# One order of work for a recurrent attention block and its gated layer: block loads as k, w, then v and r; the diagonal's first products ahead of the last key products; the fifth unit's key copies later

## The chip, the cores and the metric

The kernel runs on one core of one Trainium2 chip. The metric is device time in microseconds (us), from the start to the end of one execution. Each core has five engines with instruction streams of their own: TensorE (PE, matrix products), VectorE (DVE), ScalarE (ACT), GpSimd (POOL) and SyncE (SP, which here only issues transfers). Sixteen DMA engines move data between the chip's main memory (HBM) and the on-chip memory (SBUF). TensorE writes its results to a separate memory of eight banks (PSUM).

## What is computed

```
B, H, S, D = 4, 8, 768, 48
state = 0                                   # (B, H, D, D)
for t in range(S):
    kt, vt, rt, wt = k[:,:,t], v[:,:,t], r[:,:,t], w[:,:,t]
    cur   = outer(u * kt, vt)
    y[t]  = rt @ (state + cur)
    state = wt[..., None] * state + outer(kt, vt)
x   = y as (B*S, H*D) = (3072, 384)
h   = x @ w_in                              # (384, 2048)
out = (h * sigmoid(h)) @ w_out              # (2048, 384)
```

All data are float32. The first block is a linear attention whose state decays with `w` at every step; the second is a feed-forward layer with the SiLU function.

## The kernel before, in words

**Units.** The sequence is cut into six pieces of 128 steps and the batch into two pairs, which gives twelve units (`units`, line 66), numbered 0 to 11. For one unit the recurrence is unrolled as a tree: `tw` holds products of `w` over 1, 2, 4, ... 64 steps (`product`, line 404), the keys `tk` and queries `tr` are multiplied by them level by level (`grow_own`, `grow_keys`, `grow_queries`, lines 606 to 649), and TensorE makes scores at each level (`score_products`, line 682). Two levels at a time go to TensorE as a `burst` (line 782). The scores of the blocks of eight steps on the diagonal are made apart, on POOL by products (`block_bonus`, steps 0 to 7, line 488, all recorded as L490) and on DVE by sums (`block_sum`, recorded as L527). These sums take a way over HBM into the right layout (`block_move`, line 545).

**What a loop turn holds.** From unit 3 on, the loop at line 1428 runs the attention of unit i together with the second matrix product of unit i - 2 (`downs`, seven products of 16 matmuls each, `quarter`, line 1296, recorded as L1321) and the first matrix product of unit i - 1 (`ups`, twenty products of 16 matmuls each, `first_part`, line 1187, recorded as L1178). Both products are of the Strassen kind, with fewer products and more sums. `mix(i)` (line 958) writes this order out by hand: a list of 21 groups, each with some steps of the attention and the number of products of the feed-forward layer that follow it. Each engine takes its instructions in exactly this order (`manual_schedule`, line 78). I call the seven products q0 to q6 and the time from the `y_state` of one unit (PE, L840) to the next a unit's turn; the turn with the attention of unit i begins with the `y_state` of unit i - 1.

q0 to q6 add into three PSUM places in the order x, z, x, y, x, y, x (line 1312). A product that comes back to a place must wait until ACT (L1326) or DVE (L1329) has taken the earlier result from it, so q4 waits for ACT's copy of q2, q5 for that of q3, and q6 for DVE's sum of q4.

**Transfers.** `raw` has one room each for `w`, `r` and `k` of a unit from unit 4 on (`slot`, line 99), so a load of one unit waits until the earlier one's data were turned (`turn`, line 347, recorded as L361 on DVE). `load_blocks` (line 118, L127) brings a quarter of one of them with four transfers of 16 or 32 KB on SP; `block_loads` (line 955) lists four quarters for each of the names it is given, so that a name costs 16 transfers. `load_values` (L140, L147) has five. `load_rk` (L158) brings a second layout of `r`, `k` (issued by ACT) and `w` (by SP) for the diagonal. The attention's result goes from ACT's copies (`yt`, L866) over HBM to the layer's input: `x_out` (line 935, two transfers, L939) and `x_in` (line 942, one, L945), both issued by ACT, so that ACT's later copies stand behind them.

All transfers of SP and ACT share eight completion semaphores, which the framework gives out in turn; the built program makes each transfer wait until the one that had its semaphore before has landed, that is the one eight places ahead in the framework's order, whichever queue it is on.

**Around the change.** The lines that the change touches are 998 (unit 4), 1018 to 1038 (the groups of units 5 to 11) and 1050 to 1057 (which loads go behind which group). Before it, in a turn of a unit from 6 on, the loads of the next unit's `k` and half of its `r` stand in groups 1 to 3, and the other half of `r` and the `w` of the unit after the next stand in groups 12 to 15; in the turn of unit 5 the loads of `w` and `k` of unit 6 stand in groups 1 to 3, and `r` of unit 6 and `w` of unit 7 in groups 12 to 15. The queue of POOL in the last groups is: last key products (`go_on(i, 6)`, L639), `products_of(i + 1, 4, 5, 6)` (L407), then steps 0 to 3 of the diagonal.

Of the kernel before, what the change touches and what calls it, by code (L numbers as in the profile page):

```python
# [38 lines left out]
def kernel(  # L39
# [26 lines left out]
    units = [(n, b0) for n in range(S // L) for b0 in range(0, B, NB)]  # L66
# [885 lines left out]
    def both(fn, i, *args):  # L952
        return [(fn, i, b, *args) for b in range(NB)]
# [4 lines left out]
    def mix(i):  # L958
# [3 lines left out]
        def at(now, *steps):  # L962
            return steps if now else ()
# [4 lines left out]
        def sum_steps(j, *steps):  # L968
            return [(block_sum, j, x) for x in steps]
# [13 lines left out]
        if i < NPAIR:  # L983
            groups = [[*both(turn, i, "w"), (product, i, 0)],
                      [*both(turn, i, "k"), (odd_ones, i)], [*both(turn, i, "r"), (start_levels, i), (prepare_keys, i, 1)],
                      [(prepare, i, 1), *[(product, i, l) for l in range(1, NL)]],
                      [(burst, i, 1), (keep_level, i, 1)],
                      [(keep_level, i, 2), (go_on, i, 2)],
                      [(prepare, i, 3), (reverse_v, i), (bonus, i, 0), (bonus_sum, i, 0)],
                      [(bonus, i, 1), (burst, i, 3), (keep_level, i, 3), (bonus, i, 2)],  # L990
                      [(keep_level, i, 4), (go_on, i, 4), (bonus_sum, i, 1), (load_rk, i + 1), (load_u,)],
                      [(prepare, i, 5), (make_block_mask,), (bonus_spread, i)],
                      [(burst, i, 5), (keep_level, i, 5, 0), (keep_level, i, 6, 0), (go_on, i, 6), (bonus_write, i, (0,)), (keep_level, i, 5, 1), (keep_level, i, 6, 1), (bonus_write, i, (1,))], *end]
            groups = list(zip(groups, (1, 1, 0, 2, 1, 1, 1, 1, 1, 2, 2, 1, 1)))
        else:
            j = i - 1
            if i <= NPAIR:
                groups = [([*both(turn, i, "r"), (grow_own, i, 0), (x_out, j), *at(j >= NPAIR, (add_update, j))], 2),
                          ([*start(i), *bonus_steps(i, 4), (x_in, j), (reverse_v, i)], 1),
                          ([(grow_queries, i, 2), (sums_of_x, j, 0)], 1),  # L1000
                          ([(odd_keys, i, 2), (grow_keys, i, 2, False), (sums_of_x, j, 1)], 1),
                          ([(sums_of_x, j, 2), *sum_steps(i, 2), (prepare, i, 3), *bonus_steps(i, 5, 6, 7), (sums_of_x, j, 3, 4, 5, 6)], 2),
                          ([(burst, i, 3), (keep_level, i, 3)], 2),
                          ([*sum_steps(i, 3)], 1),
                          ([], 1),
                          ([*sum_steps(i, 4), (keep_level, i, 4)], 2),
                          ([(go_on, i, 4)], 1),
                          ([], 1),
                          ([*at(ahead, (load_rk, i + 1, (0, 1), nc.scalar)), (block_move, i, False), (block_move, i, True), *at(ahead, (load_rk, i + 1, (2,)))], 1),
                          ([], 1),  # L1010
                          ([(sums_of_x, j, 7)], 1),
                          ([(prepare, i, 5)], 2),
                          ([], 1),
                          ([(burst, i, 5), (keep_level, i, 5, 0), (keep_level, i, 6, 0), (go_on, i, 6), (block_turn, i), (block_write, i, 1)], 2),
                          ([(keep_level, i, 5, 1), (keep_level, i, 6, 1)], 1),
                          ([(block_write, i, 0)], 1),
                          (end[0], 2), (end[1], 0)]
            else:
                groups = [([*both(turn, i, "r"), (grow_own, i, 0), (x_out, j)], 2),
                          ([*at(j >= NPAIR, (add_update, j)), *start(i), *bonus_steps(i, 4), (x_in, j), (reverse_v, i)], 1),  # L1020
                          ([(odd_keys, i, 2), (grow_keys, i, 2, False), (grow_queries, i, 2), *sum_steps(i, 2)], 1),
                          ([(prepare, i, 3), *bonus_steps(i, 5), (sums_of_x, j, 0, 1)], 1),
                          ([(sums_of_x, j, 2), *bonus_steps(i, 6, 7), (sums_of_x, j, 3, 4, 5, 6)], 2),
                          ([(burst, i, 3), *sum_steps(i, 3), (keep_level, i, 3), *sum_steps(i, 4)], 2),
                          ([*at(ahead, (load_rk, i + 1, (0, 1), nc.scalar)), (block_move, i, False), (block_move, i, True), *at(ahead, (load_rk, i + 1, (2,)))], 1),
                          ([*at(ahead, *both(turn, i + 1, "w"))], 1),
                          ([(keep_level, i, 4)], 2),
                          ([(go_on, i, 4), *at(ahead, *products_of(i + 1, 0, 1, 2, 3))], 1),
                          ([], 1),
                          ([], 1),  # L1030
                          ([], 1),
                          ([(sums_of_x, j, 7)], 1),
                          ([(prepare, i, 5)], 2),
                          ([], 1),
                          ([(burst, i, 5), (keep_level, i, 5, 0), (keep_level, i, 6, 0), (go_on, i, 6), *at(ahead, *products_of(i + 1, 4, 5, 6)), (block_turn, i), (block_write, i, 1)], 2),
                          ([(keep_level, i, 5, 1), (keep_level, i, 6, 1)], 1),
                          ([(block_write, i, 0)], 1),
                          (end[0], 2), (end[1], 0)]

        if i == NPAIR:  # L1040
            groups[0][0][:0] = sum_steps(i, 0, 1)
# [4 lines left out]
        if i < NPAIR:  # L1046
            behind = [group for group, _ in groups[8:]]
            for at, group in enumerate(behind):
                group += loads[at * len(loads) // len(behind):(at + 1) * len(loads) // len(behind)]
        elif ahead:  # L1050
            blocks = block_loads(i + 1, "wkr")
            head, tail = (blocks[0:8], blocks[8:]) if i == NPAIR + 1 else (blocks[4:10], blocks[10:])
            tail += block_loads(i + 2, "w") if i + 2 < len(units) else []
            for at, some in ((1, head[0:3]), (2, head[3:5]), (3, head[5:]), (12, [(load_values, i + 1), *tail[0:1]]),
                             (13, tail[1:3]), (14, tail[3:4]), (15, tail[4:])) if i > NPAIR else ((0, blocks[0:3]), (1, blocks[3:6]), (2, [*blocks[6:8]]), (3, [(load_values, i + 1)]),
                             (12, blocks[8:9]), (13, blocks[9:10]), (14, blocks[10:11]), (15, blocks[11:])):
                groups[at][0].extend(some)
        return groups
# [421 lines left out]
```

## Time and profile before

| what | us |
|---|---|
| median of 3 runs (lowest, highest) | 585.47 (584.42, 585.62) |
| the profiled execution: its own time | 585.87 |
| its span, first to last instruction | 584.0 |
| PE busy | 561.5 (96% of the span) |
| DVE busy | 482.8 (83%) |
| POOL busy | 384.4 (66%) |
| ACT busy | 270.2 (46%) |
| mean granted PE clock | 0.994 |

The turns of units 5 to 11 begin at 211.71, 260.90, 304.01, 347.99, 391.09, 437.72 and 480.36 us of the span, and the last `y_state` is at 522.95. A turn is thus 49.2, 43.1, 44.0, 43.1, 46.6, 42.6 and 42.6 us long.

In the lists by time, a row gives the start in us, the time from the start of the first to the end of the last of its instructions, the engine ("q" behind it: its instruction queue, which issues transfers), the line, what is written from what, and how many instructions are merged. In brackets stands the engine's idle time before the row and what ended it.

### The profile page before, as it was taken

How to read it: one execution, taken by the hardware profiler on the slowest of the kernel's cores; microseconds unless marked ns; L12 is line 12 of the kernel's file. 1: busy time of each engine (PE TensorE's matmuls, PEld its weight loads, DVE VectorE, ACT ScalarE, POOL GpSimd, SP SyncE). 2: the span in 40 equal slices, each digit the busy share in tenths (PEclk: the TensorE clock that was granted, in tenths of full speed). 3: DMA queues.
4: the chain of work that ended last, by engine and by line, in shares of the span. 5: the costliest groups of instructions: out<-in, count | busy, mean ns of one | idle time of the engine just before them, and what ended most of it. 6: DMA issues, size and time to landing. Idle time of an engine off the chain costs nothing.

```text
span 584.0 us, 18864 instructions
## 1 busy us (share of the span) xinstructions
PE 561.5 (96%) x7782; PEld 520.7 (89%) x7782; DVE 482.8 (83%) x748; ACT 270.2 (46%) x604; POOL 384.4 (66%) x447
## 2 busy tenths in 40 slices
PE   8989999999999898899999999998999999999997
PEld 8767776698899898899998999998999999899997
DVE  6979799998899998789989889889779989872350
ACT  5679694531531472274273274272274272271330
POOL 5998778447799997767867767865757857710000
PEclk9999999999999999899999999998999999999999
DMA  9957775344445443455555554455365452102000
GB/s 227 307 113 199 176 245 94 47 85 104 94 84 83 108 85 61 110 86 97 115 80 100 108 85 90 108 81 100 78 108 92 92 96 56 36 5 55 28 4 25
DMA packets 206485, 57.59 MB, mean 99 GB/s; under 512 B 186048, under 2 KB 198208, under 8 KB 206400
## 3 DMA queue, kind: packets, MB, share of 16 engines
q1 hardware_dynamic: 196272, 44.01, 38.6%
q10 hardware_dynamic: 10128, 12.39, 8.1%
q8 instruction: 61, 1.00, 0.8%
q14 instruction: 24, 0.20, 0.1%
HBM read 47.14 MB, written 9.18 MB: 96 GB/s over the span
## 4 chain that ended last, share of the span: by engine, by line
PE 59%; DVE 13%; SPq 9%; POOL 7%; DMA 5%; issue 4%; ACT 1%; ACTq 1%; DVEq 0%; POOLq 0%
PE p_o L1321 19%; PE p_o L1178 12%; PE p_h L1178 8%; SPq L127 8%; PE p_h L1071 5%; PE p_m L1260 4%; POOL tk L639 2%; PE p_sc L697 2%; PE p_h L1321 2%; DVE temps L1292 2%; DMA raw<-in_w_dram 2%; POOL w_in_sb L260 2%; DVE score L715 2%; DVE block_sums L527 1%; DVE tr L621 1%
## 5 line engine op out<-in xcount | busy, mean ns | idle before, releaser
L639 POOL TENSOR_TENSOR tk<-tk,tw 128x256 f32<-128x256 f32 x128 | 96.1, 771 | 39.3 <-ACT tk L609 27.9
L1321 PE MATMUL p_o<-own,temps 128*128 128x192 f32 x528 | 90.3, 331 | 3.6 <-ACT partial L1326 3.5
L1321 PEld LDWEIGHTS p_o<-own,temps 128*128 128x128 f32 x528 | 87.6, 193 | 4.9 <-ACT partial L1326 4.5
L1178 PE MATMUL p_o<-xt,w_in_sb 128*64 128x128 f32 x1152 | 72.1, 273 | 0.7 <-POOL w_in_sb L1117 0.7
L407 POOL TENSOR_TENSOR tw<-tw 128x256 f32<-128x256 f32 (+6 forms) x83 | 42.7, 515 | 38.7 <-DVE tw L361 18.6
L1071 PE MATMUL p_h<-xt,w_in_sb 128*128 128x256 f32 x288 | 66.1, 384 | 1.7 <-POOL w_in_sb L260 1.6
L1321 PE MATMUL p_o<-w_out_sb,gt 128*128 128x192 f32 x340 | 62.1, 337 | 5.8 <-DVE ob L1329 5.1
L1178 PEld LDWEIGHTS p_o<-xt,w_in_sb 128*64 128x64 f32 x1152 | 64.7, 137 | 0.9 <-POOL w_in_sb L1117 0.9
L1321 PEld LDWEIGHTS p_o<-w_out_sb,gt 128*128 128x128 f32 x340 | 56.6, 194 | 8.1 <-DVE ob L1329 6.5
L1071 PEld LDWEIGHTS p_h<-xt,w_in_sb 128*128 128x128 f32 x288 | 53.6, 190 | 10.0 <-POOL w_in_sb L260 2.4
L490 POOL TENSOR_TENSOR ruk<-tokens_rk 128x384 f32<-128x384 f32 x48 | 53.5, 1134 | 3.8 <-DMA tokens_rk<-in_k_dram 3.8
L621 DVE TENSOR_TENSOR tr<-tr,tw 128x512 f32<-128x512 f32 x61 | 52.6, 863 | 0.7
L1326 ACT COPY partial<-p_o 128x192 f32<-128x192 f32 x33 | 10.5, 318 | 84.2 <-PE p_o L1321 59.3
L1292 DVE TENSOR_TENSOR temps<-gt 128x512 f32<-128x512 f32 (+1 forms) x48 | 44.6, 966 | 0.0
L648 POOL TENSOR_TENSOR tk<-tk,tw 128x256 f32<-128x256 f32 x32 | 25.2, 817 | 22.8 <-DVE tk L361 22.8
L609 ACT COPY tk<-tk 128x256 f32<-128x256 f32 x52 | 20.9, 402 | 40.0 <-POOL tk L639 31.2
L1202 ACT ACTIVATE gt<-p_o 128x512 f32<-128x512 f32 x45 | 26.0, 601 | 20.1 <-PE p_o L1178 20.1
L715 DVE COPY_PREDICATED score<-mask,p_sc 128x512 f32<-128x512 int8 x42 | 31.3, 801 | 2.3 <-PE p_sc L697 1.9
L1326 ACT COPY ob<-p_o 128x192 f32<-128x192 f32 x11 | 3.5, 319 | 62.9 <-PE p_o L1321 51.3
L1321 PE MATMUL p_o<-w_out_sb,temps 128*128 128x192 f32 x176 | 30.5, 327 | 0.9 <-ACT partial L1326 0.9
L1321 PEld LDWEIGHTS p_o<-w_out_sb,temps 128*128 128x128 f32 x176 | 28.8, 190 | 1.2 <-ACT partial L1326 1.2
L1205 DVE TENSOR_TENSOR p_h<-p_h,gt 128x512 f32<-128x512 f32 x27 | 18.7, 694 | 12.6 <-ACT gt L1221 12.3
(240 smaller groups left out, 1307.5 us busy)
## 6 DMA issues: line engine op xcount, KB each, us to landing
w_out_sb<-in_moe_w_in_dram SPq DMA_DIRECT2D x6, 768.0 KB, 7.3
w_out_sb<-in_moe_w_out_dram SPq DMA_DIRECT2D x4, 768.0 KB, 7.5
own<-in_moe_w_out_dram SPq DMA_DIRECT2D x4, 768.0 KB, 6.4
tokens_w<-in_w_dram SPq DMA_DIRECT2D x8, 384.0 KB, 5.2
turned<-yt ACTq DMA_DIRECT2D x16, 192.0 KB, 2.6
xt<-turned ACTq DMA_DIRECT2D x8, 384.0 KB, 3.4
tokens_rk<-in_r_dram ACTq DMA_DIRECT2D x7, 384.0 KB, 4.2
tokens_rk<-in_k_dram ACTq DMA_DIRECT2D x7, 384.0 KB, 5.7
```

Source lines behind the costliest of these rows:

```text
L127: nc.sync.dma_start(out=room[(2 * e + a) * 32:(2 * e + a + 1) * 32, :, g, 0:d1 - d0], in_=src[b0:b0 + NB, e::2, t0:t0 + 32, d0:d1].rearran ...
L407: engine.tensor_tensor(out=up, in0=t[:, :, 0::2], in1=t[:, :, 1::2], op=ALU.mult)
L490: mul = lambda out, one, two: nc.gpsimd.tensor_tensor(out=out, in0=one, in1=two, op=ALU.mult)
L621: nc.vector.tensor_tensor(out=odd, in0=odd, in1=tw[i][l][:, :, 0::2][:, :, :, None].to_broadcast([128, Q, L >> (l + 1), c]), op=ALU.mult)
L639: nc.gpsimd.tensor_tensor(out=out, in0=have, in1=odd_products(i, l, b, *blocks), op=ALU.mult)
L648: nc.gpsimd.tensor_tensor(out=have, in0=have, in1=odd_products(i, l, b, [2, NP * ni]), op=ALU.mult)
L715: nc.vector.copy_predicated(out=dst, mask=masks[l][:, :, None].to_broadcast([128, NB, NP, ni, c]), data=sc[e].rearrange("p (b q) (i c) -> ...
L1071: nc.tensor.matmul(p_h[:, a, :], lhsT=w_in_sb[:, c, f * 128:(f + 1) * 128], rhs=xt[i][:, c, :], start=(a == 0 and c == 0), stop=(a == 1 an ...
L1178: nc.tensor.matmul(p[h:h + PD, q, :], lhsT=left[:, f:f + PD], rhs=right, start=first and q == 0, stop=q == 3, skip_group_check=True)
L1202: nc.scalar.activation(out=g(f, t), in_=have, func=AF.Silu)
L1292: nc.vector.tensor_tensor(out=out, in0=one, in1=two, op=op)
L1321: nc.tensor.matmul(p, lhsT=left(f), rhs=right[:, f, :], start=which in (0, 1, 3) and f == 0, stop=f == FH - 1, skip_group_check=True)
```

## The change

- For units 5 to 10 the loads of the next unit come in the order `k`, `w`, then values, then `r`. All of `k` and `w` (32 transfers) stand in groups 1 to 3, and the values and all of `r` (5 and 16) in groups 12 to 15. The `w` of the unit after the next is no longer loaded a turn ahead. The block loads of a turn are then 48 in each of the turns 5 to 10; before they were 64 in turn 5, 48 in the turns 6 to 9 and 32 in turn 10.
- The turning of the next unit's `w` on DVE moves from group 7 to group 9, behind `go_on(i, 4)` and just ahead of the products of `w` that read it.
- On POOL step 0 of the next unit's diagonal moves ahead of the last key products, `go_on(i, 6)`; the products of `w` of levels 4 to 6 move from behind these to the end, behind the diagonal's steps 1 to 3.
- For unit 5 alone, the copies of odd keys, the key products and the sums of level 2 move one group later (behind q3), and `prepare(i, 3)` goes from group 3 to group 4, behind the third of the sums of x; for units 6 to 11 these keep their order.
- For unit 4 a step that was empty there is taken out.

```diff
-                groups = [([*both(turn, i, "r"), (grow_own, i, 0), (x_out, j), *at(j >= NPAIR, (add_update, j))], 2),
+                groups = [([*both(turn, i, "r"), (grow_own, i, 0), (x_out, j)], 2),
...
+                soon = i > NPAIR + 1
+                keys_2 = [(odd_keys, i, 2), (grow_keys, i, 2, False), *at(soon, (grow_queries, i, 2)), *sum_steps(i, 2)]
+                keys_3 = [(prepare, i, 3), *bonus_steps(i, 5)]
...
-                          ([(odd_keys, i, 2), (grow_keys, i, 2, False), (grow_queries, i, 2), *sum_steps(i, 2)], 1),
-                          ([(prepare, i, 3), *bonus_steps(i, 5), (sums_of_x, j, 0, 1)], 1),
-                          ([(sums_of_x, j, 2), *bonus_steps(i, 6, 7), (sums_of_x, j, 3, 4, 5, 6)], 2),
+                          ([*at(not soon, (grow_queries, i, 2)), *at(soon, *keys_2)], 1),
+                          ([*at(soon, *keys_3), *at(not soon, *keys_2), (sums_of_x, j, 0, 1)], 1),
+                          ([(sums_of_x, j, 2), *at(not soon, *keys_3), *bonus_steps(i, 6, 7), (sums_of_x, j, 3, 4, 5, 6)], 2),
...
-                          ([*at(ahead, *both(turn, i + 1, "w"))], 1),
+                          ([], 1),
                           ([(keep_level, i, 4)], 2),
-                          ([(go_on, i, 4), *at(ahead, *products_of(i + 1, 0, 1, 2, 3))], 1),
+                          ([(go_on, i, 4), *at(ahead, *both(turn, i + 1, "w"), *products_of(i + 1, 0, 1, 2, 3))], 1),
...
-                          ([(burst, i, 5), (keep_level, i, 5, 0), (keep_level, i, 6, 0), (go_on, i, 6), *at(ahead, *products_of(i + 1, 4, 5, 6)), (block_turn, i), (block_write, i, 1)], 2),
+                          ([(burst, i, 5), (keep_level, i, 5, 0), (keep_level, i, 6, 0), *at(ahead, *bonus_steps(i + 1, 0)), (go_on, i, 6), (block_turn, i), (block_write, i, 1)], 2),
...
-                          (end[0], 2), (end[1], 0)]
+                          ([*at(ahead, *bonus_steps(i + 1, 1, 2, 3)), *at(ahead and i > NPAIR, *products_of(i + 1, 4, 5, 6))], 2),
+                          (end[1], 0)]
...
-            blocks = block_loads(i + 1, "wkr")
-            head, tail = (blocks[0:8], blocks[8:]) if i == NPAIR + 1 else (blocks[4:10], blocks[10:])
-            tail += block_loads(i + 2, "w") if i + 2 < len(units) else []
-            for at, some in ((1, head[0:3]), (2, head[3:5]), (3, head[5:]), (12, [(load_values, i + 1), *tail[0:1]]),
-                             (13, tail[1:3]), (14, tail[3:4]), (15, tail[4:])) if i > NPAIR else ((0, blocks[0:3]), (1, blocks[3:6]), (2, [*blocks[6:8]]), (3, [(load_values, i + 1)]),
+            blocks = block_loads(i + 1, "wkr" if i <= NPAIR else "kwr")
+            for at, some in ((1, blocks[0:3]), (2, blocks[3:6]), (3, blocks[6:8]), (12, [(load_values, i + 1), *blocks[8:9]]),
+                             (13, blocks[9:10]), (14, blocks[10:11]), (15, blocks[11:])) if i > NPAIR else ((0, blocks[0:3]), (1, blocks[3:6]), (2, [*blocks[6:8]]), (3, [(load_values, i + 1)]),
```

## The prediction

> **What bounds the kernel now.** I read the page's table of busy time first (PE at 96% of the span), then looked in the list of PE's work by time for idle stretches, then at whoever ended each.
>
> ```profile
> PE   561.5 (96%) x7782; PEld 520.7 (89%) x7782; DVE 482.8 (83%) x748; ACT 270.2 (46%) x604; POOL 384.4 (66%) x447
> ```
>
> PE's list, turns 5, 7, 9 and 10 in that order:
>
> ```profile
> 229.70 2.87 PE L1321 MATMUL p_o<-w_out_sb,temps 128*128 128x192 f32 x16 [0.95 <-ACT partial L1326]
> 235.17 4.55 PE L1321 MATMUL p_o<-w_out_sb,gt 128*128 128x192 f32 x16 [2.60 <-DVE ob L1329]
> ...
> 314.21 8.07 PE L1321 MATMUL p_o<-own,temps 128*128 128x192 f32 x48 [1.27 <-ACT partial L1326]
> ...
> 402.26 9.75 PE L1321 MATMUL p_o<-own,temps 128*128 128x192 f32 x48 [2.25 <-ACT partial L1326]
> ...
> 446.48 7.96 PE L1321 MATMUL p_o<-own,temps 128*128 128x192 f32 x48
> 457.45 2.87 PE L1321 MATMUL p_o<-w_out_sb,gt 128*128 128x192 f32 x16 [0.41 <-DVE ob L1329]
> ```
>
> PE waits only in the first half of a turn: in turns 7 and 9 before q2, for ACT's copy of q0; in turn 5 before q5 and q6; and before q6, for DVE, by 0.41, 0.40 and 0.41 us in turns 6, 8 and 10 and by 1.24 us in turn 11. The row at 402.26 also runs slow: 9.75 us where turn 10 takes 7.96. The windows' table tells why; its first number behind the length is PE's busy time, and PEclk stands behind POOL's:
>
> ```profile
> 399.97:403.39 3.42, 1.17 (x8) 1.13 (x8) 3.39 (x6) 1.50 (x7) 3.42 (x5) 1.00 0.69 121
> 403.39:406.80 3.41, 3.41 (x12) 3.41 (x11) 3.37 (x8) 0.69 (x4) 1.60 (x2) 0.50 0.61 142
> ```
>
> After a stretch in which PE was busy for 1.17 of 3.42 us, the clock was 0.50 in the next. The same happened in turn 5 (0.96 busy, then 0.50), not in turn 7 (2.14 busy, then 1.00).
>
> Why is ACT late in turn 9? ACT's list and SP's list:
>
> ```profile
> 393.28 2.36 ACT L866 COPY yt<-p_m 48x512 f32<-48x512 f32 x4 [0.98 <-PE p_m L861]
> 398.52 3.33 ACTq L939 DMA_DIRECT2D turned<-yt  x2
> 401.89 0.32 ACT L1326 COPY partial<-p_o 128x192 f32<-128x192 f32 x1 [6.25 <-DMA raw<-in_w_dram]
> ...
> 385.37 5.39 SPq L127 DMA_DIRECT2D raw<-in_r_dram  x8
> 390.86 9.92 SPq L127 DMA_DIRECT2D raw<-in_w_dram  x16
> 400.88 8.28 SPq L127 DMA_DIRECT2D raw<-in_k_dram  x16
> ```
>
> The copies of `yt` end at 395.64, but the two stores behind them (x_out) issue at 398.52 and 401.54: each shares a semaphore with a load of `w` that SP is still issuing. The built program names them, the 9th and the 13th of the 16 loads of `w`. ACT's copy of q0 stands behind, and PE behind that.
>
> **The change part by part.** The sum is made against the profiled execution, 585.87 us, which is 0.40 above the median.
>
> *Order of loads, turns 6 to 9 (start).* Behind the values SP now issues 16 loads of `r`; the 8 + 16 of `r` and `w` become 16. In the built program x_out waits for the 11th and the 14th of them. In turn 9 an `r` load took 5.39 / 8 = 0.67 us of issue; the 14th goes at 385.37 + 13 x 0.67 = 394.1 and lands some 2.1 us later (the median of the page's row for `r`), at 396.2. That is 0.6 us behind the copies of `yt` and before q0 ends (397.25), so ACT is ready. Turn 9 loses its 2.25 us wait and the slow clock, 9.75 - 7.96 = 1.79: 4.04 us. Turn 7 loses 1.27. In turns 6, 8 and 10 x_out is late too, but PE does not wait for it. Bounds: all of the 5.31, or only half of it if landings slip by 2 us; I take all, since the queue is 8 loads (5 us) shorter at this point.
>
> The Trainium skill (TensorE: Matmul & The Clock Gate, section Why this matters for your kernels) lets the clock fall only for idle gaps of over about 3 us; by it the 2.25 us of turn 9 would cost no clock and the sum would be 1.79 us smaller. The trace does not agree: 0.50 was granted after a gap of 2.25 us.
>
> *What takes its place.* `x_in` now waits for the 4th load of `k` in turns 6 to 10 (in turn 10 it waited for the 2nd, by the built program). In turn 10 the first went 9.04 us after the `y_state` (446.76 after 437.72), the 4th 1.35 later, plus 2.1 to land: 12.5. ACT's copy of q2 stands behind and must be done when q3 ends, 14.1 after the `y_state` (three products to 454.28 from 446.48, less one). Slack 1.2 us: cost 0, up to 1 us per turn if a landing takes 4 us, as `vq` does on the page.
>
> *The w loads between k and ACT's load_rk.* In turns 6 to 10 there are now 32 loads before it instead of 24, as turn 5 already had; load_rk of `k` waits for the 14th `w`, the 30th load. Turn 5 issued its 32 at 0.53 us (221.72 to 238.82), so the 30th goes 9.0 + 29 x 0.53 = 24.5 after the `y_state` and lands at 26.6; with 0.56 us of issue ACT goes on at 27.2. In turn 10 ACT's next copy began at 465.36, 27.6 after, and PE did not wait. Cost 0 by this, 0.45 by turn 5, whose long issue of 1.80 us left a PE wait of 0.45. Five turns, 0 to 2.25; I take 0.1 each, 0.5.
>
> *Turning w later.* 1.29 us on DVE move behind L621 (425 in turn 9), into an idle 1.40 before the sum at 426.12, which waits for ACT. The four products of `w` on POOL (2.55 us) follow at 426.0 instead of 421.3, and the key products of level 5 behind them end at 429.8 instead of 426.3. PE's level 6 scores need them at 431.1: slack 1.3, in turn 10 (DVE 1.1 later) 0.2. Cost 0; without that cover 0 to 1 us a turn. The loads of `w` land at about 28, two us before DVE turns them.
>
> *Step 0 of the diagonal first.* POOL's list of turn 9:
>
> ```profile
> 425.12 1.20 POOL L639 TENSOR_TENSOR tk<-tk,tw 128x256 f32<-128x256 f32 x2
> 429.90 1.19 POOL L639 TENSOR_TENSOR tk<-tk,tw 128x256 f32<-128x256 f32 x2 [3.58 <-ACT tk L609]
> 431.05 0.24 POOL L407 TENSOR_TENSOR tw<-tw 128x32 f32<-128x32 f32 x1
> 432.83 1.42 POOL L407 TENSOR_TENSOR tw<-tw 128x16 f32<-128x16 f32 x2 [1.54 <-DVE spare L560]
> ```
>
> Its idle 3.58 and 1.54 are filled by 1.96 us of step 0 and by work that no longer waits. The last key products end at 433 instead of 431.1; PE transposes them at 437.1. POOL ends its part at 441.0 instead of 442.44. This matters to DVE, which makes q6 wait: its sums L1292 take 1.49 us beside POOL and 0.68 alone. The fourth, 1.31 at 441.68, becomes 0.68, a gain of 0.63. Against it, the first L566 takes 1.36 beside the products of `w` and would take 2.09 beside L490, as the second does; 0.3 of that reaches L1292. Net 0.3 a turn (ends -0.3 and +0.63): 0.9 in turns 6, 8 and 10, 0.3 in turn 11, less 0.2 for the 0.1 wait at q6 that turns 7 and 9 then show. 1.0 us.
>
> *Unit 5.* ACT's copy of q3 no longer stands behind the odd keys, which wait for POOL until 229.00; the 0.95 before q5 goes. But q6 waits for DVE's L1329, behind the sums L527 that POOL releases at 231.37; only L776 (0.65) leaves this path. PE stands at q6 for 3 us instead, and gains 0.65. Whether the half clock behind it (4.55 for 2.87, 1.68 us) stays depends on where the 3.41 us stretches fall; I let it stay.
>
> Sum: 4.04 + 1.27 - 0.5 + 1.0 + 0.65 = 6.5; 585.87 - 6.5 = 579.4, and 579.0 against the median.
>
> **Rivals.**
> - *Partial gain.* x_in holds ACT, or POOL beside DVE gives nothing back. At 1 us in four of the turns, or 1.0 less and half of 5.31 kept: 579.0 + 3 or so, 582. For it: landings of 4 us exist; against it: 1.2 us of slack.
> - *Slower: load_rk becomes ACT's wait.* Place: L158 in turns 6 to 10. If the 32 loads take 0.62 us each, the 30th lands at 9.0 + 18.0 + 2.2 = 29.2, ACT goes on at 29.8, 2.2 late, 11 us in five turns: 590. It decides from 0.58 us on (then 1.3 late in each, all the gain). For it: tails of turns 6 to 9 run at 0.60 to 0.70 an issue; against it: all heads run at 0.49 to 0.57.
> - *No change.* x_out still late because the tail starts later, and DVE bounds the first half: 585.5. Little speaks for it, the queue being shorter.
>
> **How the numbers follow.** About 0.2% (1.2 us) is what a measurement of this kernel can tell from no change. Forecast (575 to 581) 0.59, partial gain (581 to 584) 0.17, no change (584 to 586.6) 0.07, slower 0.17: its price is large and it sits only 0.05 us per load above the rate of turn 5. So faster 0.76, same 0.07, slower 0.17. Down, the range takes in 1.68 for the clock of turn 5, 0.5 for load_rk and 1.3 if POOL gives back its full 0.63, together 575.5, so 575. Up it reaches through the partial gain and no change to 586.6; only the slower case, 0.17, lies outside. The likeliest case alone spans 575 to 581.
>
> **What would show it.** x_out within 1 us of the last copy of `yt` in turns 6 to 10; no wait before q2 and no half clock in turn 9; L407 of levels 4 to 6 as POOL's last; q6 waits of 0.1 instead of 0.4; turn 5 with its wait before q6 alone. Wrong would be a wait of PE behind L158, a later L697, or ACT idle behind L945.

## The result and the profile after

| what | before | changed |
|---|---|---|
| median (lowest, highest), us | 584.94 (584.25, 585.62) | 577.88 (576.23, 578.62) |
| ratio of the times, 95% interval | | 0.9875 (0.985 to 0.9901) |
| span of the profiled execution, us | 584.0 | 576.8 |
| mean granted PE clock | 0.994 | 0.997 |

The change is 7.06 us faster, where 6.5 was forecast. The page's table of busy time hardly moves (PE 561.5 to 558.9 us, its share 96% to 97%):

```profile
PE 558.9 (97%) x7782; PEld 518.0 (90%) x7782; DVE 482.5 (84%) x748; ACT 270.8 (47%) x604; POOL 394.8 (68%) x447
```

The gain is idle time and half clock, so it is read by turns, from one `y_state` (L840) to the next in PE's list:

| turn | 5 | 6 | 7 | 8 | 9 | 10 | 11 | sum |
|---|---|---|---|---|---|---|---|---|
| before | 49.19 | 43.11 | 43.97 | 43.10 | 46.64 | 42.63 | 42.60 | 311.24 |
| changed | 47.48 | 42.79 | 42.77 | 43.63 | 43.29 | 42.56 | 42.28 | 304.80 |
| difference | -1.71 | -0.32 | -1.20 | +0.53 | -3.35 | -0.07 | -0.32 | -6.44 |

Another 0.72 us lie ahead of turn 5, all of it before the `y_state` of unit 2 (118.53 to 117.79 us), where the change touches nothing; that point lay anywhere from 117.5 to 122.0 us in the runs below. The end, from the last `y_state` on, takes 61 us in both. PE's list of the changed kernel, turns 5 and 8 to 11:

```profile
225.34 2.87 PE L1323 MATMUL p_o<-own,temps 128*128 128x192 f32 x16 [0.23 <-ACT partial L1328]
233.41 4.55 PE L1323 MATMUL p_o<-w_out_sb,gt 128*128 128x192 f32 x16 [2.60 <-DVE ob L1331]
...
353.49 8.07 PE L1323 MATMUL p_o<-own,temps 128*128 128x192 f32 x48 [0.53 <-ACT partial L1328]
...
396.43 8.01 PE L1323 MATMUL p_o<-own,temps 128*128 128x192 f32 x48
...
440.25 8.07 PE L1323 MATMUL p_o<-own,temps 128*128 128x192 f32 x48 [0.36 <-ACT partial L1328]
...
493.05 2.87 PE L1323 MATMUL p_o<-w_out_sb,gt 128*128 128x192 f32 x16 [0.92 <-DVE ob L1331]
```

(Line numbers behind the edit are two higher: L1323 is the L1321 of before, L1328 its L1326, L1331 its L1329, L1294 its L1292, L1207 its L1205.) The waits before q2 in turns 7 and 9 are gone, and q2 to q4 of turn 9 run in 8.01 us instead of 9.75. The q6 waits of turns 6 and 10 are gone, turn 8 keeps 0.10 and turn 11's fell from 1.24 to 0.92. New are 0.53 and 0.36 before q2 in turns 8 and 10, again for ACT. In turn 5 the 0.95 before q5 went, 0.23 before q4 came, the 2.60 before q6 stayed, and so did its half clock.

Is ACT free now? ACT's list of turn 9 says no, only less late:

```profile
389.87 2.37 ACT L866 COPY yt<-p_m 48x512 f32<-48x512 f32 x4 [0.18 <-PE p_m L861]
392.85 3.11 ACTq L939 DMA_DIRECT2D turned<-yt  x2
396.00 0.32 ACT L1328 COPY partial<-p_o 128x192 f32<-128x192 f32 x1 [3.76 <-DMA raw<-in_r_dram]
```

`yt` is done at 392.24, and ACT stands until 396.00 for loads of `r`: 8.3 us after the `y_state`, where q2 starts at 8.8. SP's list tells where these 3.8 us come from. Turn 8 into 9 of before, then of the changed kernel:

```profile
374.05 0.33 SPq L549 DMA_DIRECT2D kept<-block_sums  x1
378.30 0.38 SPq L554 DMA_DIRECT2D spare<-kept  x1
```

```profile
372.10 0.47 SPq L549 DMA_DIRECT2D kept<-block_sums  x1
377.15 0.38 SPq L554 DMA_DIRECT2D spare<-kept  x1
...
383.01 12.03 SPq L127 DMA_DIRECT2D raw<-in_r_dram  x16
```

Counted from the turn's `y_state` (347.99 and 344.03), the move of the sums (L549) starts 26.1 us in before and 28.1 after: eight more loads now stand ahead of it. L554, which reads what L549 wrote, goes when that has landed, 4.2 us behind L549 in before and 5.1 behind it after. The loads of `r` therefore start 4.7 us ahead of the next `y_state`, not 5.7 (385.37 against 391.09).

In turns 6, 7 and 9 the landing weighs more than the later start. ACT's two loads of load_rk (L158) are issued at about the same time; here their second rows, of before and of the changed kernel:

```profile
374.33 0.56 ACTq L158 DMA_DIRECT2D tokens_rk<-in_k_dram  x1
```

```profile
370.83 1.18 ACTq L158 DMA_DIRECT2D tokens_rk<-in_k_dram  x1
```

In turns 7 and 9 of before L549 went ahead of both, and L554 followed 1.5 us later; in turns 6, 8 and 10 it went between the two, and L554 followed 4.2 us later; in turns 6 to 10 of the changed kernel it goes behind both, and L554 follows 4.7 to 6.8 us later. Turns 5 to 10 of all fourteen profiles agree: 1.5 to 3.4 us ahead of both (23 cases), 4.0 to 5.2 between them (23 of 24, one at 1.55), 3.5 to 7.1 behind both (37). In the changed kernel the last loads of `w` stand just ahead of L549 too, and no run moves L549 or load_rk alone, so the reason is not tested.

### The profile page after: what moved, and what is told of

The parts are those of the page before. It is cut to its first block, busy times and chain, and to the rows that moved or that the text cites. A ratio compares the mean times of both kernels' runs of the same rounds, so it can differ in the third digit from the quotient of the medians.

```text
span 576.8 us, 18839 instructions
## 1 busy us (share of the span) xinstructions
PE 558.9 (97%) x7782; PEld 518.0 (90%) x7782; DVE 482.5 (84%) x748; ACT 270.8 (47%) x604; POOL 394.8 (68%) x447
## 4 chain that ended last, share of the span: by engine, by line
PE 49%; DVE 15%; SPq 13%; DMA 9%; POOL 7%; issue 4%; ACT 2%; ACTq 0%; DVEq 0%; POOLq 0%
PE p_o L1323 14%; SPq L127 11%; PE p_o L1180 11%; PE p_h L1180 7%; PE p_h L1073 4%; PE p_m L1262 4%; DVE temps L1294 3%; PE p_sc L697 2%; POOL tk L639 2%; DMA raw<-in_k_dram 2%; PE p_h L1323 2%; POOL w_in_sb L260 2%; DVE tr L621 2%; DMA kept<-block_sums 2%; DMA raw<-in_r_dram 1%
## 5 line engine op out<-in xcount | busy, mean ns | idle before, releaser
L639 POOL TENSOR_TENSOR tk<-tk,tw 128x256 f32<-128x256 f32 x128 | 105.0, 841 | 18.3 <-ACT tk L609 8.0
L1323 PE MATMUL p_o<-own,temps 128*128 128x192 f32 x528 | 88.8, 327 | 1.2 <-ACT partial L1328 1.1
L1323 PEld LDWEIGHTS p_o<-own,temps 128*128 128x128 f32 x528 | 85.8, 190 | 2.6 <-ACT partial L1328 2.2
L407 POOL TENSOR_TENSOR tw<-tw 128x256 f32<-128x256 f32 (+6 forms) x83 | 45.4, 546 | 48.2 <-DVE tw L361 44.3
L1323 PE MATMUL p_o<-w_out_sb,gt 128*128 128x192 f32 x340 | 62.1, 337 | 4.3 <-DVE ob L1331 3.5
L1323 PEld LDWEIGHTS p_o<-w_out_sb,gt 128*128 128x128 f32 x340 | 56.5, 194 | 6.6 <-DVE ob L1331 5.1
L490 POOL TENSOR_TENSOR ruk<-tokens_rk 128x384 f32<-128x384 f32 x48 | 53.6, 1138 | 4.2 <-DMA tokens_rk<-in_k_dram 4.2
L621 DVE TENSOR_TENSOR tr<-tr,tw 128x512 f32<-128x512 f32 x61 | 54.1, 886 | 0.7
L1328 ACT COPY partial<-p_o 128x192 f32<-128x192 f32 x33 | 10.4, 319 | 80.4 <-PE p_o L1323 43.8
L1294 DVE TENSOR_TENSOR temps<-gt 128x512 f32<-128x512 f32 (+1 forms) x48 | 44.7, 969 | 0.0
L648 POOL TENSOR_TENSOR tk<-tk,tw 128x256 f32<-128x256 f32 x32 | 25.2, 820 | 16.1 <-DVE tk L361 16.1
L1328 ACT COPY ob<-p_o 128x192 f32<-128x192 f32 x11 | 3.5, 319 | 59.8 <-PE p_o L1323 53.8
L1323 PE MATMUL p_o<-w_out_sb,temps 128*128 128x192 f32 x176 | 30.4, 326 | 0.0
L490 POOL TENSOR_TENSOR spare<-tokens_rk 128x384 f32<-128x384 f32 x24 | 29.0, 1221 | 0.6
L1323 PE MATMUL p_h<-w_out_sb,gt 128*128 128x192 f32 x168 | 29.1, 326 | 0.0
```

Of the source, the lines that this page charges most:

```text
L407: engine.tensor_tensor(out=up, in0=t[:, :, 0::2], in1=t[:, :, 1::2], op=ALU.mult)
L490: mul = lambda out, one, two: nc.gpsimd.tensor_tensor(out=out, in0=one, in1=two, op=ALU.mult)
L621: nc.vector.tensor_tensor(out=odd, in0=odd, in1=tw[i][l][:, :, 0::2][:, :, :, None].to_broadcast([128, Q, L >> (l + 1), c]), op=ALU.mult)
L639: nc.gpsimd.tensor_tensor(out=out, in0=have, in1=odd_products(i, l, b, *blocks), op=ALU.mult)
L648: nc.gpsimd.tensor_tensor(out=have, in0=have, in1=odd_products(i, l, b, [2, NP * ni]), op=ALU.mult)
L1294: nc.vector.tensor_tensor(out=out, in0=one, in1=two, op=op)
```

## The experiments

Three questions: which part gives what; whether x_out is the price, or the order of loads itself; and whether the two findings make a still faster kernel. Ratios are to the kernel before, run on the same chip, with 95% intervals. The turns come from the one profiled execution of each run.

| run | ratio | 5 | 6 | 7 | 8 | 9 | 10 | 11 |
|---|---|---|---|---|---|---|---|---|
| e_order | 0.9903 (0.9866 to 0.9939) | 48.66 | 43.15 | 43.15 | 43.71 | 43.21 | 42.73 | 42.64 |
| e_loads_alone | 1.0053 (1.0016 to 1.0091) | 48.56 | 47.32 | 43.74 | 44.02 | 43.45 | 43.73 | 42.61 |
| e_diag_unit5 | 0.992 (0.9891 to 0.9949) | 47.59 | 43.26 | 49.10 | 42.62 | 42.62 | 42.12 | 41.32 |
| e_diag | 0.9898 (0.986 to 0.9937) | 48.69 | 42.63 | 49.14 | 43.53 | 42.62 | 42.01 | 41.31 |
| after_again | 0.9875 (0.9835 to 0.9915) | 46.44 | 43.24 | 42.90 | 42.80 | 42.89 | 42.71 | 42.25 |
| x_pool_before | 1.0041 (1.0016 to 1.0067) | 48.37 | 44.41 | 43.86 | 43.84 | 44.42 | 43.93 | 43.22 |
| e_diag_turnw | 0.9898 (0.9849 to 0.9946) | 48.60 | 42.76 | 43.97 | 43.41 | 42.50 | 41.93 | 41.68 |
| b_gp_t5 | 0.9891 (0.9845 to 0.9937) | 49.80 | 42.43 | 42.88 | 44.14 | 43.30 | 42.29 | 41.94 |
| x_early_before | 0.9902 (0.9872 to 0.9931) | 48.94 | 43.11 | 43.12 | 43.11 | 43.15 | 42.63 | 42.61 |
| best_early | 0.989 (0.9854 to 0.9926) | 48.75 | 44.28 | 43.84 | 42.63 | 42.69 | 41.99 | 41.31 |
| after_early | 0.9876 (0.9847 to 0.9906) | 48.38 | 42.44 | 42.69 | 42.97 | 42.77 | 43.26 | 42.27 |
| best_xin | 0.9956 (0.9923 to 0.9988) | 47.94 | 43.80 | 46.42 | 42.62 | 44.05 | 43.96 | 41.32 |

### The order of loads, with and without the later turning

`e_order` puts only these two hunks of the change into the kernel before:

```diff
-            blocks = block_loads(i + 1, "wkr")
-            head, tail = (blocks[0:8], blocks[8:]) if i == NPAIR + 1 else (blocks[4:10], blocks[10:])
...
+            blocks = block_loads(i + 1, "wkr" if i <= NPAIR else "kwr")
...
-                          ([*at(ahead, *both(turn, i + 1, "w"))], 1),
+                          ([], 1),
...
-                          ([(go_on, i, 4), *at(ahead, *products_of(i + 1, 0, 1, 2, 3))], 1),
+                          ([(go_on, i, 4), *at(ahead, *both(turn, i + 1, "w"), *products_of(i + 1, 0, 1, 2, 3))], 1),
```

> Before, with the new order of loads and the later turning of w (they belong together); the diagonal and unit 5 stay as before. My theory: the order of loads is most of the change, through x_out, behind which ACT's copy of q0 stands. The waits before q2 in turns 7 and 9 (1.26 and 2.25) and the half clock of turn 9 (1.7) go, 5.2 us; turns 8 and 10 get the waits of 0.5 and 0.4 that the changed kernel shows. So 0.6 to 0.9% faster, ratio 0.991 to 0.994; the q6 waits of 0.4 in turns 6, 8 and 10 stay. Rival: the gain comes from the shorter DVE sums beside POOL; then this kernel is within 0.3% of the kernel before.

Measured: 0.9903. The waits before q2 in turns 7 and 9 and the half clock of turn 9 are gone; the q6 waits are 0.45, 0.41, 0.51 and 0.43 us in turns 6, 7, 9 and 10 and 1.28 in turn 11. The waits expected before q2 in turns 8 and 10 did not show; in turn 8 PE waits 0.33 us for a sum of DVE (L1203) instead. Against the rival, the load order works alone, and without shorter sums on DVE (8.5 to 9.3 us a turn from turn 6 on).

`e_loads_alone` is the first of the two hunks alone.

> Before, with the new order of loads only; w is turned where it was, in group 7. In the changed kernel the last load of w is issued 25.2 us after the y_state in turn 10 and so lands at about 27.3; the turning stood at 25 in the kernel before. If the moved turning is there because of the loads, DVE stands some 2 to 3 us at L361 in turns 6 to 10, and the sums for the first product behind it hold PE by 1 to 2 us a turn: 0.4% faster to 0.8% slower, clearly behind the run with both. Rival: the loads land in time or DVE's slack covers it; then it equals the run with both within 0.2%.

Measured: 1.0053. DVE's list and PE's list in turn 6:

```profile
288.77 1.30 DVE L361 STREAM_TRANSPOSE tw<-raw 128x512 f32<-128x512 f32 x2 [3.29 <-DMA raw<-in_w_dram]
290.00 0.67 DVE L1203 TENSOR_TENSOR p_o<-gt,p_h 128x512 f32<-128x512 f32 x1
```

```profile
290.72 1.39 PE L1176 MATMUL p_o<-gt,in_sum 128*64 128x128 f32 x16 [2.18 <-DVE p_o L1203]
```

DVE stands 3.29 us for the last loads of `w`, the sum L1203 behind it is late, and PE waits 2.18. The later turning is there for the loads: without it the order of loads costs more than it gives.

### The rest of the change, and the diagonal alone

```diff
-(keep_level, i, 6, 0), (go_on, i, 6), *at(ahead, *products_of(i + 1, 4, 5, 6)), (block_turn, i), (block_write, i, 1)], 2),
+(keep_level, i, 6, 0), *at(ahead, *bonus_steps(i + 1, 0)), (go_on, i, 6), (block_turn, i), (block_write, i, 1)], 2),
...
-                          (end[0], 2), (end[1], 0)]
+                          ([*at(ahead, *bonus_steps(i + 1, 1, 2, 3)), *at(ahead and i > NPAIR, *products_of(i + 1, 4, 5, 6))], 2),
+                          (end[1], 0)]
```

This is `e_diag`; `e_diag_unit5` adds the lines on `soon`, `keys_2` and `keys_3`.

> All but the loads and the turning of w: the diagonal's step 0 ahead, products of w last on POOL, and unit 5's keys later. My theory: the x_out waits and the half clock of turn 9 stay (5.2 us); the q6 waits of 0.41, 0.40, 0.41 in turns 6, 8 and 10 go and turn 11's falls by 0.3 (1.5 us together); turn 5 gives 1.0 (its wait before q5 goes, q6 comes 1.04 earlier). Together 2.5 us, ratio 0.9957 (0.994 to 0.997). Rival: without the load order these gain nothing (ratio 0.999 to 1.001), or, were they the main part, 0.990.

> The diagonal's order on POOL alone. My theory: 1.5 us from the q6 waits of turns 6, 8, 10 and 11, ratio 0.9974 (0.996 to 0.9985); DVE's fourth sum L1292 falls from 1.31 to 0.69 in every turn from 6 on, with POOL ending no earlier than before (4.7 to 5.6 us after the y_state), because the small products L407 that now stand last do not slow DVE. Rival: the fourth sum stays at 1.31, so the shorter sums come from something else, ratio 1.000.

Measured: 0.992 and 0.9898, far more than the 0.9974 expected of the diagonal. Unit 5's lines shorten turn 5 by 1.10 us (48.69 to 47.59); for the rest the two agree within their intervals. The profiled execution of `e_diag` is the longest of its seven (584.37 us, median 580.06), and so is that of `e_diag_unit5`: in their turn 7 x_out is held longer than in the kernel before (3.65 and 3.06 us of wait, each with two stretches at half clock). The other turns show what was not expected. DVE's list and POOL's list of `e_diag` around the `y_state` at 438.13:

```profile
437.76 1.33 DVE L1293 TENSOR_TENSOR temps<-gt 128x512 f32<-128x512 f32 x2
439.01 0.68 DVE L1293 TENSOR_TENSOR temps<-temps,gt 128x512 f32<-128x512 f32 x1
439.80 0.69 DVE L1293 TENSOR_TENSOR temps<-gt,temps 128x512 f32<-128x512 f32 x1
```

```profile
434.73 1.95 POOL L490 TENSOR_TENSOR tokens_rk<-tokens_rk,tokens_w 128x384 f32<-128x384 f32 x1
436.63 2.52 POOL L407 TENSOR_TENSOR tw<-tw 128x32 f32<-128x32 f32 x3
```

POOL ends 1.0 us after the `y_state` instead of 4.7, and all eight sums of DVE take 0.7 us: 5.5 together, not 8.5 (6.3 in turns 7 and 8). DVE no longer makes q6 wait, and turn 11 falls to 41.31 us.

DVE's sums are not all of it. The largest gain of this profile is turn 9's, 4.02 us (46.64 to 42.62): the wait before q2 and the half clock are gone, with every load where it was. ACT's list (`y_state` at 395.51):

```profile
399.71 3.89 ACTq L939 DMA_DIRECT2D turned<-yt  x2
403.64 0.32 ACT L1327 COPY partial<-p_o 128x192 f32<-128x192 f32 x1 [3.51 <-DMA raw<-in_w_dram]
```

x_out's second store went 7.8 us after the `y_state`, not 10.5. The loads of `w`, for which it waits, started 2.5 us ahead of the `y_state`, not 0.2: in turn 8 L549 went just ahead of load_rk, and L554 followed it by 1.8 us instead of 4.2. The diagonal alone thus takes away lateness of x_out that the order of loads was to take away; `e_diag_unit5` and `e_diag_turnw` have the same in turns 8 and 9. That L549's place is the reason is read from the traces, not tested.

`e_diag_turnw` adds the later turning of `w` to `e_diag`, to see whether that is what holds POOL in the changed kernel.

> The diagonal's order on POOL and the later turning of w, without the order of loads. With the diagonal alone POOL ended 1.0 us after the y_state and DVE's eight sums took 5.5 us instead of 8.5. My new theory: the later turning holds POOL's products of w and the key products behind them, so that POOL ends at 4 to 5.6 us again, the sums take 7.1 to 7.9 us as in the changed kernel, and turns 10 and 11 last 42.4 to 42.6 and 42.2 us instead of 42.0 and 41.3. Rival: DVE's sums stay at 5.5 us and it was the order of loads that held POOL.

Measured: POOL ends 4.9 to 5.6 us after the `y_state` in turns 6 to 10 and the sums take 7.9 us, as expected and as in the changed kernel. POOL's list around the `y_state` at 433.82:

```profile
435.42 1.34 POOL L490 TENSOR_TENSOR tokens_rk<-tokens_rk,tokens_w 128x384 f32<-128x384 f32 x1
436.72 2.06 POOL L407 TENSOR_TENSOR tw<-tw 128x32 f32<-128x32 f32 x3
```

So the later turning costs POOL four microseconds a turn. But turns 10 and 11 last 41.93 and 41.68, not 42.4 and 42.2, and the ratio is 0.9898 again: as long as the fourth sum and those behind it are short, 2.4 us more on DVE reach PE only in turn 11 (0.32 before q6). Half of the theory falls: the mechanism is there, its price is small.

### Is x_out the price?

`x_pool_before` leaves loads, turning and POOL's products alone and lets POOL's queue issue the two stores that stood in ACT's way:

```diff
-                groups = [([*both(turn, i, "r"), (grow_own, i, 0), (x_out, j)], 2),
+                groups = [([*both(turn, i, "r"), (grow_own, i, 0), (x_out, j, nc.gpsimd)], 2),
```

> Before, with the two stores x_out of units 6 to 11 issued by POOL's queue instead of ACT's; nothing else is changed. My theory says that what costs the time in turns 7 and 9 is ACT standing at x_out until loads of w have landed, not the order of loads as such. Then ACT's copy of q0 goes at 6.2 to 6.5 us after the y_state in every turn, the waits of 1.26 and 2.25 before q2 and the half clock of turn 9 are gone (5.2 us in the profile), and the q6 waits of 0.4 stay: ratio 0.990 to 0.995. Rival: the stores wait for the same loads on POOL and hold its products, and the turns get longer (ratio 1.000 or above).

Measured: 1.0041, slower. POOL's list and ACT's list of turn 8 (`y_state` at 348.39):

```profile
356.88 1.65 POOL L648 TENSOR_TENSOR tk<-tk,tw 128x256 f32<-128x256 f32 x2 [3.78 <-DVE tk L361]
358.48 1.18 POOL L939 DMA_DIRECT2D turned<-yt  x2
```

```profile
362.33 0.40 ACTq L945 DMA_DIRECT2D xt<-turned  x1
362.78 0.32 ACT L1326 COPY partial<-p_o 128x192 f32<-128x192 f32 x1 [5.90 <-PE p_o L1321]
```

The run was badly placed: at this point of the order POOL's queue already holds the key products, which wait for DVE, so x_out goes 10 us after the `y_state`, x_in waits for its landing, and ACT's copy of q2 stands behind x_in. PE then waits before q4, 0.6 to 1.9 us in the turns 6 to 11 and 3.6 in turn 5. Which queue waits for whom, not the order of loads, made this kernel slower; but it did not test x_out. So the stores were moved to right behind the copies of `yt`, where POOL is just done:

```diff
-(y_state, i), *both(y_values, i), *at(ahead, *turns(i + 1))
+(y_state, i), *both(y_values, i), *at(ahead and i >= NPAIR, (x_out, i, nc.gpsimd)), *at(ahead, *turns(i + 1))
...
-                groups = [([*both(turn, i, "r"), (grow_own, i, 0), (x_out, j)], 2),
+                groups = [([*both(turn, i, "r"), (grow_own, i, 0)], 2),
```

> Before, with x_out of units 4 to 10 on POOL's queue again, but placed right behind the copies of yt, ahead of the next unit's products. (In the run before this, POOL issued x_out at 10 us after the y_state, since the key products L648 stood ahead of it, and x_in went at 14.) My theory is still that ACT standing at x_out behind loads of w is the price: x_out now goes at 4.7 to 6 us, when POOL ends, x_in at 9 to 12.5, no wait before q2 in turns 7 and 9 and no half clock there; q6 waits of 0.4 to 0.7 stay. 4 to 5 us in a run like the one profiled, ratio 0.990 to 0.996. Rival: x_in, which still shares a semaphore with loads, holds ACT instead, and the wait moves from q2 to q4 (ratio 0.998 to 1.005).

Measured: 0.9902, the gain of the whole load order, with every load where it was. Turn 9 in POOL's list, ACT's and PE's (`y_state` at 389.14):

```profile
393.82 1.18 POOL L939 DMA_DIRECT2D turned<-yt  x2
```

```profile
395.50 0.32 ACT L1326 COPY partial<-p_o 128x192 f32<-128x192 f32 x1 [1.80 <-PE p_o L1321]
```

```profile
397.90 7.96 PE L1321 MATMUL p_o<-own,temps 128*128 128x192 f32 x48
408.91 2.87 PE L1321 MATMUL p_o<-w_out_sb,gt 128*128 128x192 f32 x16 [0.45 <-DVE ob L1329]
```

ACT copies q0 as soon as PE ends it, no turn from 6 on waits before q2, and turns 6 to 9 all last 43.1 us with the same q6 wait of 0.4. So ACT standing at x_out is the price that the order of loads removes.

### Can the parts be put together better?

`after_again` is the changed kernel on the chip of the next runs.

> The changed kernel once more, so that it stands beside the others on one chip: ratio 0.9875 again (0.984 to 0.991).

Measured: 0.9875, as before. `b_gp_t5` takes the diagonal and unit 5 with the loads and the turning of before, x_out on POOL as in `x_pool_before`, and in turn 5 moves the sums of level 2, at which DVE waits for POOL, behind DVE's sum of q4:

```diff
-keys_2 = [(odd_keys, i, 2), (grow_keys, i, 2, False), *at(soon, (grow_queries, i, 2)), *sum_steps(i, 2)]
+keys_2 = [(odd_keys, i, 2), (grow_keys, i, 2, False), *at(soon, (grow_queries, i, 2), *sum_steps(i, 2))]
...
-([(sums_of_x, j, 2), *at(not soon, *keys_3),
+([(sums_of_x, j, 2), *at(not soon, *sum_steps(i, 2), *keys_3),
```

> The diagonal's order and unit 5 of the change, without the load order and the later turning; x_out of units 6 to 11 on POOL's queue; and in turn 5 the sums of level 2 (L527, which wait for POOL) behind the third sum of x, so that L1329 of q4 goes ahead of them. If the parts are understood: turn 5 loses its wait of 2.6 us before q6 and the half clock of 1.7 us, less about 1 us of new wait at the scores behind; turns 6 to 9 last 42.6 us, turn 10 42.1, turn 11 41.3, as in the undisturbed turns of the run with the diagonal alone. That is 45 + 4 x 42.6 + 42.1 + 41.3 = 298.8 for turns 5 to 11, where the kernel before has 311.2 and the changed one 304.8: ratio 0.979 (0.975 to 0.985), 1% below the changed kernel. Rival: other waits take the place of these, ratio 0.987 or above.

Measured: 0.9891, where 0.975 to 0.985 was expected. The wait before q6 in turn 5 is gone, but x_out stood behind POOL's products and PE waited 3.57 us before q4 instead. `best_early` and `after_early` repeat it with x_out in the place of `x_early_before`, on the loads of before and on those of the change.

> The diagonal's order and unit 5 of the change, the loads and the turning of w as before, x_out on POOL's queue behind the copies of yt, and in turn 5 the sums L527 of level 2 behind L1329 of q4. POOL ends 1.0 us after the y_state in this order, so x_out goes as soon as yt is there (3.4 and 4.6) and lands by 8. Turn 5 loses the wait of 2.6 before q6 and the half clock (45 to 46 us), turns 6 to 9 last 42.6, 10 and 11 42.1 and 41.3: ratio 0.979 (0.975 to 0.985). Rival: x_in is held by loads of k at 12 to 14, ratio 0.986 or above.

> The changed kernel with the same two additions (x_out on POOL behind the copies of yt, turn 5's sums L527 later). POOL ends at 5.0 to 5.6 us after the y_state here, behind the products L407, so x_out goes at 5.0 to 6.8 instead of 6.6 to 8.7; the waits before q2 of turns 8 and 10 (0.53, 0.36) go, turn 5 loses some 3 us: ratio 0.981 (0.978 to 0.986), 0.6% below the changed kernel. Rival: ACT was not held by x_out for the worse here, and only turn 5 gains, ratio 0.983 to 0.988.

Measured: 0.989 and 0.9876, outside both ranges; neither is below the changed kernel. Turn 5 of `best_early`, PE's list, then ACT's and POOL's:

```profile
231.22 2.87 PE L1325 MATMUL p_o<-w_out_sb,gt 128*128 128x192 f32 x16 [1.23 <-DVE ob L1333]
...
243.39 1.98 PE L1182 MATMUL p_o<-gt,in_sum 128*64 128x128 f32 x16 [2.82 <-DVE p_o L1209]
```

```profile
240.46 0.55 ACTq L158 DMA_DIRECT2D tokens_rk<-in_r_dram  x1
...
241.70 0.58 ACT L1203 COPY gt<-p_o 128x512 f32<-128x512 f32 x1 [4.00 <-POOL tk L639]
```

```profile
238.45 1.98 POOL L490 TENSOR_TENSOR ruk<-tokens_rk 128x384 f32<-128x384 f32 x2
```

The wait before q6 fell to 1.23, and a wait of 2.82 came twelve microseconds later (1.30 and 2.50 in `after_early`). ACT's load_rk overwrites `tokens_rk`, which POOL reads until 240.43, and a copy and a sum for PE stand behind it. So POOL's diagonal paces turn 5 in these runs: the edit moved the wait and did not remove it.

In turn 7 of `best_early` x_in held ACT until 14.3 us after the `y_state` and cost 0.94. `best_xin` leaves the sums of level 2 of turn 5 where the change has them and puts x_in behind ACT's copy of q2:

```diff
-([*at(j >= NPAIR, (add_update, j)), *start(i), *bonus_steps(i, 4), (x_in, j), (reverse_v, i)], 1),
-([*at(not soon, (grow_queries, i, 2)), *at(soon, *keys_2)], 1),
+([*at(j >= NPAIR, (add_update, j)), *start(i), *bonus_steps(i, 4), (reverse_v, i)], 1),
+([*at(not soon, (grow_queries, i, 2)), *at(soon, *keys_2), (x_in, j)], 1),
```

> The diagonal's order and unit 5 of the change, loads and turning of w as before, x_out on POOL's queue behind the copies of yt, and x_in behind ACT's copy of q2 (in the run before, x_in held that copy in turn 7 until 14.3 us after the y_state, 0.94 of wait). The sums L527 of turn 5 stay where the change puts them: moving them later took the wait before q6 down to 1.22 us, and gave 2.82 of wait for L1209 behind it, since POOL ends the diagonal of turn 5 no earlier. Turn 5 then lasts 47.5 us as in the changed kernel, turns 6 to 9 42.6 to 43.0, turn 10 42.0 and turn 11 41.3; 302 us for turns 5 to 11, where the changed kernel has 304.8: ratio 0.983 (0.980 to 0.987). Rival: POOL's gain is spent by waits for w and load_rk in the turns from 6 on, ratio 0.988 or above, no better than the change.

Measured: 0.9956. Where x_in held ACT it now holds DVE. Turn 7, DVE's list and PE's list:

```profile
321.63 0.71 DVE L1143 TENSOR_TENSOR xt<-xt 128x256 f32<-128x256 f32 x1 [3.48 <-DMA xt<-turned]
322.37 1.10 DVE L1146 TENSOR_TENSOR gt<-xt 128x256 f32<-128x256 f32 x1
323.50 0.36 DVE L1333 TENSOR_TENSOR ob<-p_o,partial 128x192 f32<-128x192 f32 x1
```

```profile
323.91 2.52 PE L1325 MATMUL p_o<-w_out_sb,gt 128*128 128x192 f32 x11 [1.87 <-DVE ob L1333]
```

The sums of x wait for the transfer, the sum of q4 stands behind them, and PE waits before q6 by 0.6 to 1.9 us in four turns. No run was faster than the change.

## Right and wrong, step by step

- **Order of loads, turns 7 and 9.** Right in mechanism and nearly in size: 1.20 instead of 1.27 in turn 7, and 3.99 of wait and clock in turn 9 (2.25 and 1.74, 4.04 forecast), of which 0.6 came back; 0.29 of that is a wait at the turn's end (L566 stood 1.13 us for the move of the sums, and PE waited for the L1207 behind it). That ACT at x_out is the cause is shown by `x_early_before`. The lateness that remains was mis-sized. "The queue is 8 loads (5 us) shorter at this point" overlooked that the same eight loads now stand ahead of the move of the sums, which also lands later, and so ahead of the tail. In turn 9 the 14th load of `r` was issued 4.4 us after the `y_state`, not 3.0, and landed 3.5 us later, not 2.1; in turns 7, 8 and 10 it was issued 6.1 to 6.8 us after. x_out's second store went 8.0 to 8.7 us after the `y_state` in turns 7 to 10, where "within 1 us of the last copy of `yt`" was forecast, and turns 8 and 10 lost 0.53 and 0.36. That belongs to the rival of a partial gain; it took 0.9 of 5.3.
- **x_in.** Right: 12.2 to 12.6 us after the `y_state` in turns 6 to 10 (12.5 forecast), and no wait of PE behind it. The slack was smaller than the 1.2 us of the forecast, which left out x_in's own issue of 0.4. In turn 5, where x_in goes at 13.5, PE waits 0.23 before q4.
- **load_rk.** The 0.5 us was not lost: it went at 25.4 to 26.2, PE did not wait for it, and the 32 loads took 0.53 to 0.56 us each, below the 0.58 from which the slower rival would have decided. (By the prediction's own terms 0.58 makes ACT 1.0 us late, not 1.3, and the whole gain is spent at 0.59.)
- **Step 0 first, and the q6 waits.** The size was close (1.4 us in turns 6, 8, 10 and 11, where 1.2 was forecast, and the 0.2 set against it for turns 7 and 9 did not show), the reason half wrong. POOL did not end 1.4 us earlier but 0.2 to 0.9 later in turns 6 to 9 (5.0 to 5.6 us after the `y_state`) and 11; in turn 10 it ended 0.7 earlier, at 4.0. The fourth sum fell from 1.31 to 0.69 in all of them, as what POOL does last is now the small L407. The rows of turn 10, the first four sums and POOL's end:

```profile
430.56 2.91 DVE L1294 TENSOR_TENSOR temps<-gt 128x512 f32<-128x512 f32 x2
433.38 0.72 DVE L1294 TENSOR_TENSOR temps<-temps,gt 128x512 f32<-128x512 f32 x1
434.21 0.69 DVE L1294 TENSOR_TENSOR temps<-gt,temps 128x512 f32<-128x512 f32 x1
```

```profile
431.57 1.34 POOL L490 TENSOR_TENSOR tokens_rk<-tokens_rk,tokens_w 128x384 f32<-128x384 f32 x1
432.86 2.10 POOL L407 TENSOR_TENSOR tw<-tw 128x32 f32<-128x32 f32 x3
```

  Sums beside L490 take 1.5, beside L407 of 128x32 or smaller 0.7. The Trainium skill (SBUF — State Buffer, section Who interferes with whom) says that a DVE instruction with two SBUF inputs and a GpSimd instruction that reads SBUF block each other for a whole instruction; the rows agree, in that the long products cost a sum 0.8 us and the short ones next to nothing.
- **Turning w later, "cost 0".** PE lost little by it, as forecast, but the step hid a gain: without it POOL ends 4 us earlier and DVE saves 2.4 us a turn (`e_diag` against `e_diag_turnw`).
- **Unit 5.** 0.65 was forecast and turn 5 gained 1.71. Of this, 1.10 is unit 5's edit (two runs agree on it: q6 comes 1.04 earlier in the changed kernel, 0.65 from L776 and 0.41 from a sum of x that took 0.45 instead of 0.86). Most of the rest is the wait of 0.45 before L1178, which went, as the issue of load_rk for `k` took 0.55 us instead of 1.80. Why that issue is shorter is open: turn 5 of `e_order` lasts 48.66 us with an issue of 1.31, but `e_diag` and `e_diag_turnw`, with the loads of before, have 48.69 and 48.60 with 0.92 and 1.35. That second wait was in the trace of before (the prediction's "PE waits only in the first half of a turn" passes over it) and was not counted as something to gain.
- **The sum.** The parts don't add. The load order alone gives 0.97%, the diagonal alone 1.02%, the change 1.25%; these intervals overlap, and it is the turns that tell the cases apart. Each alone already takes away turn 9's wait before q2 and its half clock, 4 us that the forecast gave to the load order, and a wait that one has removed can't be removed again.
- **Luck in the total.** That 6.5 and 7.06 lie so close is in part luck. The load order gave some 3.7 us in turns 7 to 10 (1.20 and 3.35, less 0.53 and 0.36) instead of 5.3; unit 5 gave 1.1 more than forecast, load_rk cost 0.5 less, the q6 waits gave 0.4 more, and 0.7 of the profiled gain lies ahead of turn 5, in no term of the sum.

## What to carry to other kernels

When a store or load on a compute engine's queue shares completion semaphores with a stream of loads elsewhere, as x_out does here, that stream can set its issue time; look for the engine's copies behind it, and try first to issue it from a queue that is idle at that moment. Moving loads from one end of a queue to the other shortens one wait and lengthens what they now stand ahead of: count both. A small transfer that its own queue waits for, like L549, deserves a look at what is issued just ahead of it. Parts that remove waits in the same stretch of a loop are not summed; a run of each alone says what is left for the other.

## What the runs showed of the hardware

The half clock goes by fixed stretches of 3.41 us, not by the length of a gap. In turn 7 of `best_xin` a wait of 1.87 us was followed by one, in turn 5 of `after_again` a longer one of 2.66 was not. The windows' table of `best_xin`, then of `after_again`:

```profile
321.95:325.36 3.41, 1.54 (x10) 1.45 (x10) 3.31 (x5) 0.00 (x0) 3.41 (x4) 1.00 0.41 51
325.36:328.78 3.42, 3.42 (x40) 2.98 (x42) 1.99 (x6) 0.32 (x1) 0.11 (x1) 0.50 0.34 80
```

```profile
228.61:232.03 3.42, 2.67 (x17) 2.38 (x15) 1.56 (x6) 0.41 (x1) 3.42 (x5) 1.00 0.31 39
232.03:235.44 3.41, 1.50 (x9) 1.50 (x10) 3.34 (x8) 0.92 (x2) 3.25 (x5) 1.00 0.38 47
235.44:238.85 3.41, 3.41 (x91) 3.12 (x91) 2.12 (x5) 0.32 (x1) 3.33 (x5) 1.00 0.41 52
```

Where the 2.66 falls across a boundary, neither stretch is idle enough. In all fourteen profiles every change of the granted clock lies on one grid of such stretches. Between 20 and 570 us, from a clock of 1.00, the sixteen stretches in which PE was busy for 0.2 to 1.4 us were all followed by 0.50 and those above 1.9 by 1.00; between 1.5 and 1.9 both occur (1.50 and 1.54 above went one way each), so PE's busy time alone doesn't settle it there. From a clock of 0.50 more was needed: 2.3 to 2.7 us of busy time were followed by another half stretch (turn 7 of `e_diag` and `e_diag_unit5`, turn 5 of `b_gp_t5`), 3.0 and more by 1.00 in all twenty cases. Where the wait falls on the stretches is what makes turn 5 of `after_again` last 46.44 us and that of the changed kernel's first profile 47.48, although the waits of `after_again` are 0.4 longer. The Trainium skill (TensorE: Matmul & The Clock Gate, Part 1: The HAM clock gate) describes the window of 3413 ns as free-running, and the traces agree; its case of a whole idle window is not needed, since 1.87 us of idle time were enough.

One such stretch costs 1.7 us (q6 of turn 5 takes 4.55 us instead of 2.87) and takes 0.003 off the mean clock of an execution. The 19 executions of the kernel before beside `e_order` have mean clocks from 0.997 down to 0.988 and times from 581.92 to 589.75 us; the four at 0.988 are all above 588.5. With x_out early, all six executions lie between 578.15 and 580.53, at clocks of 0.997 or 1.0. That the waits for landings set the spread as well as the time fits this, but six executions don't show it.
